# One recorded order for all five engines after the first transform of a spectral filter and two-layer expert kernel

## The chip, the cores and the metric

The kernel runs on one core of a Trainium2 chip. The metric is the device time in microseconds (us) of one execution. TensorE (PE) multiplies matrices into PSUM; VectorE (DVE), ScalarE (ACT) and GpSimd (POOL) do the elementwise work; SyncE (SP) and ACT issue nearly all transfers. Each engine takes its instructions from its own queue in order.

## The reference

Eight sequences of 3072 tokens with 256 channels go through three stages (cut to what matters):

```python
X = np.fft.rfft(x, axis=1)                        # spectral filter, per batch and channel
y = np.fft.irfft(X * (filt_r + 1j * filt_i), n=3072, axis=1)
y_prev = shift y by one token                      # zero at the start
xk = mu_k * y + (1 - mu_k) * y_prev;  xr = mu_r * y + (1 - mu_r) * y_prev
x2 = sigmoid(xr @ w_r) * (np.maximum(xk @ w_k, 0) ** 2 @ w_v)      # d_ff 1024
h = maximum(x2 @ w1, x2 @ w2, x2 @ w3)                             # 768 wide
out = h @ w_out
```

## The kernel before

**Stages.** The first batch's transform (`fft_first`) stands alone at the start, on an order written by hand. After it the tokens are worked through in 64 chunks of 384 tokens (eight a batch) and 32 pairs of chunks. Every large product is made of three matmuls on high and low parts, 384 columns wide.

- `kv(i)` is the list of steps for chunk i: `r_mm` (12 matmuls and a sigmoid), eight times `k_mm` (6 matmuls; then ACT relu `kr`, DVE square, ACT cast `khi`, POOL subtraction `klo`) and, three steps behind (`LAG`), eight times `v_mm` (6 matmuls that read `khi`, `klo` and a streamed weight tile `ws`). `x2` multiplies by the gate.
- `y_load` and `y_mm` fetch a chunk of transformed data and make its inputs `xh`, `xl`.
- `combos(p)` makes seven combinations of a pair; `second(p)` is nine `block`s of seven products (`one` to `seven`, 3 matmuls each, PSUM tiles `pb`, `pa`, `pe`) that feed a running maximum `m`, split into `hh`. `o_mm` (6 matmuls of 256 columns) multiplies `hh` by w_out, six calls for each third of the blocks; three `po` tiles gather them over the pair.
- `fft(b)` is the transform of batch b = 1 to 7, done beside the chunks of batch b-1: 17 steps `pa` that load x, add or subtract on DVE and call `a_mm1` or `a_mm0`, then steps that load (`b_load`), multiply (`b_mm`), filter on ACT, DVE and POOL (`b_filt`), multiply back (`c_mm`) and store (`c_out`) for six groups u. These matmuls use a quarter of the array each (64 by 64), in `quarters`: 126 groups over the run (42 of `b_mm`, 42 of `c_mm`, 28 of `a_mm1`, 14 of `a_mm0`), each with two PSUM tiles. Ahead of a group DVE copies one element into each of its two PSUM tiles (line 493), so that DVE takes the wait for the bank.
- During the first chunks `wjobs2` converts the weights of the expert stage (ACT, DVE, POOL, matmuls `ps`, stores).

**Order.** `drive` deals the steps of `fft(b)` out among the steps of the chunks by weights written beside each step. What it yields is only a program order: a list scheduler with a timeline of its own then sets each engine's order, from priorities and a general cost model; only the matmuls of `quarters` are raised in priority and chained. PSUM has eight banks in one pool `ps`, which all matmul tiles share.

Of the kernel before, what the change touches and what calls it, by code (L numbers as in the profile page):

```python
# [1 line left out]

# [214 lines left out]
def drive(main, side, total_main, total_side):  # L217

    done_m = 0.0
    done_s = 0.0  # L220
    i = 0
    for w, fn in main:
        fn()
        done_m += w
        while i < len(side) and done_s * total_main < done_m * total_side:
            side[i][1]()
            done_s += side[i][0]
            i += 1
    while i < len(side):
        side[i][1]()  # L230
        i += 1
# [3 lines left out]
def tile_spectral_moe(ctx: ExitStack, tc, x, xr, xz, filt, ones, wa, wa1, wi, wbc, wb1, wc1, filt1, filt0, mu, w_k, w_v, w_r, w1, w2, w3, w_out, out):  # L235
# [17 lines left out]
    fp = ctx.enter_context(tc.tile_pool(name="fp", bufs=2))  # L253
    ws = ctx.enter_context(tc.tile_pool(name="ws", bufs=10))
    dp = ctx.enter_context(tc.tile_pool(name="dp", bufs=2, space=bass.MemoryType.DRAM))
# [3 lines left out]
    ps = ctx.enter_context(tc.tile_pool(name="ps", bufs=8, space=bass.MemoryType.PSUM))  # L259
# [176 lines left out]
    def fft(b):  # L436
# [6 lines left out]
        pieces = []  # L443

# [42 lines left out]
        def quarters(o, of, whole=False):  # L487

            last = None
            for y in range(2):  # L490
                _, d = of(y, 1, 1)
                d = d[:1, 0, :1] if whole else d[:1, :1]
                i = nc.vector.tensor_copy(o[y][y * H : y * H + 1, 0, :1], d)
                if y:
                    tc.add_manual_dep(i.ins, last, ORDER_ONLY, reason="banks")
                last = i.ins.name
            last = None
            for k in range(1 if whole else 2):
                for y in (1, 0):
                    for x in range(2):  # L500
                        w, d = of(y, x, k)
                        to = o[y][x * H : x * H + H] if whole else o[y][x * H : x * H + H, k]
                        with tc.high_priority():
                            i = mm(to, w, d, k == 0, True, True, (y * H, x * H))
                        if last is not None:
                            tc.add_manual_dep(i.ins, last, ORDER_ONLY, reason="quarters")
                        last = i.ins.name
# [5 lines left out]
        NBS = NG // 2  # L513
        for u in range(len(jobs) + 1):
            def pa(u=u):
                if u == 0:
                    jobs[0][0](*jobs[0][2:])
                if u + 1 < len(jobs):
                    jobs[u + 1][0](*jobs[u + 1][2:])
                if u < len(jobs):  # L520
                    jobs[u][1](*jobs[u][2:])
                if u:
                    _, what, t, x = jobs[u - 1]
                    if x and what is a_diff:
                        a_mm1(t)
                    elif x and t % 2:
                        a_mm0(t - 1)
            pieces.append((0.53, pa))
# [53 lines left out]
        for u in range(NU4 + 2):  # L582
            def pb(u=u):
                if u < NU4:
                    b_load(u)
                if 1 <= u <= NU4:
                    b_mm(u - 1)
                    b_filt(u - 1, 0)
            def pb2(u=u):
                if 1 <= u <= NU4:  # L590
                    b_filt(u - 1, 1)
            def pc(u=u):
                if u >= 2:
                    c_mm(u - 2)
                    c_out(u - 2, 0)
            def pc2(u=u):
                if u >= 2:
                    c_out(u - 2, 1)
            pieces.append((0.4, pb))
            pieces.append((0.7, pb2))  # L600
            if u == 0:

                pieces.append((7.7, lambda: None))
            pieces.append((0.4, pc))
            pieces.append((0.7, pc2))
        return pieces
# [183 lines left out]
    mp = ctx.enter_context(tc.tile_pool(name="mp", bufs=2))  # L790
# [214 lines left out]
    def kv(i, before=()):  # L1005

        u = []
        before = list(before)
        at = [later(wv_d[f // 2][:, f % 2], 2, C) for f in range(NF)]
        add = lambda w, fn, *a: u.append((w, lambda: fn(*a)))  # L1010

        def some(n):
            while before and n:
                u.append(before.pop(0))
                n -= 1

        if i > 0:
            add(1.95, r_mm, i)
        direct = i + 1 < NTOT and (i in (0, 2) or i % 2 == 1 and i != 3)
        for f in range(NF):  # L1020
            add(0.98, k_mm, i, f)
            some(1)
            if f == 0 and direct:
                add(0.0, y_load, i + 1)
            if f == 4 and direct:
                add(1.3, y_mm, i + 1)
            if f >= LAG:
                add(0.98, v_mm, i, f - LAG, at[f - LAG])
        for f in range(NF - LAG, NF):
            add(0.98, v_mm, i, f, at[f])  # L1030
        some(len(before))
        if i == 0:
            add(1.95, r_mm, i)
        add(0.0, x2, i)
        return u

    def second(p):

        u = []
        add = lambda w, fn, *a: u.append((w, lambda: fn(*a)))  # L1040
        nb = NB
        i = 2 * p + (3 if p else 4)
        todo = []

        at = [{} for _ in range(nb)]

        def ask(k, a, e):
            i = later(wu_d[k][:, a:e], e - a, 2, P)
            at[k].update({n: (i, n - a) for n in range(a, e)})

        for k in range(nb + 1):
            if k < nb:
                ask(k, 0, 2)
            if k:
                ask(k - 1, 4, 5)
            if k < nb:
                ask(k, 2, 4)
            if k:
                ask(k - 1, 5, 7)
        for k in range(nb):  # L1060
            if k == 1 and i < NTOT:
                add(0.0, y_load, i)
            if k and k % 3 == 0:
                todo = [lambda q=q, fq=k // 3 - 1: o_mm(p, fq, q) for q in range(2 * NTB)]
            now = block(p, k, at[k])
            for n, fn in enumerate(now):

                u.append((0.52, fn))
                if n in (0, 2, 3) and k:
                    u.append((0.52, late.pop(0)))  # L1070
                if todo and n in ((3,), (0, 2, 3), (0, 1))[k % 3]:
                    u.append((0.71, todo.pop(0)))
                if n == 3:
                    break
            late = now[4:]
            if k == nb - 3 and i < NTOT:
                add(1.3, y_mm, i)
        for fn in late:
            u.append((0.52, fn))
        return u, [(0.71, lambda q=q: o_mm(p, NU // 2 - 1, q)) for q in range(2 * NTB)]  # L1080


    kv0 = kv(0)
# [15 lines left out]
    units = kv0 + kv(1) + kv(2) + [(0.0, lambda: combos(0))] + kv(3)  # L1099
    marks, cuts = {}, {}  # L1100
    before2 = len(units)
    s, left = second(0)
    units += s
    units.append((0.0, lambda: combos(1)))
    for p in range(1, NPAIR):
        i = 2 * p + 2
        if i < NTOT:
            if i % NCH == 0:
                marks[i // NCH] = len(units)
            units += kv(i, left if p == 1 else ())  # L1110
        s, left = second(p)
        units += s
        if i + 1 < NTOT:
            if (i + 2) % NCH == 0:
                cuts[i // NCH] = len(units)
            end = i + 2 == NTOT
            units += kv(i + 1, () if end else left)
            units.append((0.0, lambda p=p: combos(p + 1)))
            if end:
                units += left  # L1120
# [3 lines left out]
    for k, fn in enumerate(wjobs2):  # L1124
        units.insert(min(3 + int(k * (before2 - 3) / (NB + 1.5)), before2 + 10 + 3 * (k - NB)) + k, (0.0, fn))
    units.insert(20, (0.0, lambda: tc.keep_in_program_order(nc.gpsimd.dma_start(wa_s, wa))))
    n2 = len(wjobs2) + 1

    lead = before2 + n2
    starts = [0] + [marks[b] + n2 for b in range(1, B)]  # L1130
    ends = starts[1:] + [len(units)]
    for b in range(B):
        part = units[starts[b] : ends[b]]
        if b + 1 < B:
            side = fft(b + 1)
            cut = cuts[b] + n2 - starts[b]
            if b == 0:
                for _, fn in part[:lead]:
                    fn()
                part, cut = part[lead:], cut - lead  # L1140
            drive(part[:cut], side, sum(w for w, _ in part[:cut]), sum(w for w, _ in side))
            for _, fn in part[cut:]:
                fn()
        else:
            for _, fn in part:
                fn()
# [47 lines left out]
```

## Time and profile before

| | |
|---|---|
| median of 3 runs | 3155.18 us (3153.65 to 3156.64) |
| the profiled execution | 3154.04 us |
| its span in the trace | 3152.3 us |
| first transform ends, weights of the chunks warm up | 81 us |
| last matmul starts | 3146.14 us |
| transfers | 660 MB, mean 209 GB/s |

The profiled execution is 1.1 us under the median, and 1.7 us over its span. A busy share of PE is to be read with care: matmuls overlap, and a matmul's recorded length (340 ns) is near twice the step from one to the next, so a PE that waits a little still shows as busy.

### The profile page before, as it was taken

How to read it: one execution, taken by the hardware profiler on the slowest of the kernel's cores; microseconds unless marked ns; L12 is line 12 of the kernel's file. 1: busy time of each engine (PE TensorE's matmuls, PEld its weight loads, DVE VectorE, ACT ScalarE, POOL GpSimd, SP SyncE). 2: the span in 40 equal slices, each digit the busy share in tenths (PEclk: the TensorE clock that was granted, in tenths of full speed). 3: DMA queues.
4: the chain of work that ended last, by engine and by line, in shares of the span. 5: the costliest groups of instructions: out<-in, count | busy, mean ns of one | idle time of the engine just before them, and what ended most of it. 6: DMA issues, size and time to landing. Idle time of an engine off the chain costs nothing.

```text
span 3152.3 us, 56835 instructions
## 1 busy us (share of the span) xinstructions
PE 3075.5 (98%) x19816; PEld 2914.4 (92%) x19816; DVE 1872.8 (59%) x3313; ACT 1877.1 (60%) x3901; POOL 1626.9 (52%) x1416
## 2 busy tenths in 40 slices
PE   8799999999999999999999999999999999999998
PEld 5788989999989989999999998999999999999998
DVE  7875675466655666456655576545665456545554
ACT  6555655566555665556656566565655566655554
POOL 5433654457544565446645465455654466544443
PEclk9899999999999999999999999999999999999999
DMA  7777677666776666767767577775776666555554
GB/s 240 228 243 237 206 264 241 193 184 215 252 228 196 202 218 216 245 179 221 233 214 217 174 228 233 227 223 167 226 258 228 189 187 213 169 164 171 160 166 122
DMA packets 385195, 660.24 MB, mean 209 GB/s; under 512 B 41473, under 2 KB 150177, under 8 KB 384625
## 3 DMA queue, kind: packets, MB, share of 16 engines
q1 hardware_dynamic: 319584, 581.94, 59.9%
q10 hardware_dynamic: 64720, 72.52, 6.7%
q8 instruction: 160, 2.62, 0.3%
q0 software_dynamic: 608, 2.16, 0.2%
q14 instruction: 123, 1.00, 0.1%
HBM read 573.75 MB, written 82.71 MB: 208 GB/s over the span
## 4 chain that ended last, share of the span: by engine, by line
PE 78%; DVE 9%; DMA 4%; POOL 4%; issue 3%; ACT 2%; SPq 0%; ACTq 0%; POOLq 0%; DVEq 0%
PE pb L262 18%; PE pv L262 13%; PE pk L262 12%; PE po L262 12%; PE pe L262 8%; PE pa L262 5%; PE pr L262 4%; PE py L262 3%; POOL klo L290 2%; PE pc L262 1%; DMA ws<-wud 1%; DMA xr<-in_xr 1%; DVE filt L559 1%; DVE sc L887 1%; DVE m L970 1%
## 5 line engine op out<-in xcount | busy, mean ns | idle before, releaser
L290 POOL TENSOR_TENSOR hh<-m,hh 128x384 fp32r<-128x384 f32 x384 | 407.5, 1070 | 829.9 <-ACT hh L289 629.2
L262 PE MATMUL pb<-x,ws 128*128 128x384 f32 x3456 | 768.9, 340 | 13.5 <-DMA ws<-wud 6.7
L290 POOL TENSOR_TENSOR klo<-kr,khi 128x384 fp32r<-128x384 f32 x492 | 522.7, 1070 | 311.6 <-ACT khi L289 287.4
L262 PEld LDWEIGHTS pb<-x,ws 128*128 128x128 f32 x3456 | 597.1, 189 | 56.4 <-issue 13.6
L855 DVE SCALAR_TENSOR_TENSOR kr<-pk,kr 128x384 f32<-128x384 f32 x512 | 281.0, 553 | 365.3 <-ACT kr L854 363.4
L262 PE MATMUL pv<-khi,ws 128*128 128x384 f32 x2048 | 483.4, 338 | 14.2 <-ACT khi L289 11.3
L262 PE MATMUL po<-wo_hi,hh 128*128 128x256 f32 x2304 | 480.6, 283 | 4.8 <-ACT hh L289 4.0
L262 PEld LDWEIGHTS po<-wo_hi,hh 128*128 128x128 f32 x2304 | 389.0, 189 | 12.4 <-ACT hh L289 7.3
L262 PE MATMUL pe<-x,ws 128*128 128x384 f32 x1728 | 390.0, 339 | 2.4 <-DVE sc L969 1.2
L289 ACT CAST khi<-kr 128x384 fp32r<-128x384 f32 x512 | 261.1, 513 | 215.2 <-DVE kr L855 200.0
L262 PEld LDWEIGHTS pv<-khi,ws 128*128 128x128 f32 x2048 | 358.6, 188 | 30.8 <-ACT khi L289 16.5
L262 PE MATMUL pk<-xh,wk_hi 128*128 128x384 f32 x1024 | 341.4, 338 | 3.6 <-ACT xh L289 3.3
L262 PE MATMUL pk<-xh,wk_lo 128*128 128x384 f32 x1024 | 343.9, 336 | 0.0
L262 PE MATMUL pk<-xl,wk_hi 128*128 128x384 f32 x1024 | 343.1, 335 | 0.0
L854 ACT ACTIVATE kr<-pk 128x384 f32<-128x384 f32 x512 | 249.9, 490 | 124.1 <-POOL klo L290 57.7
L262 PE MATMUL po<-wo_lo,hh 128*128 128x256 f32 x1152 | 315.9, 281 | 0.0
L262 PE MATMUL pv<-klo,ws 128*128 128x384 f32 x1024 | 300.1, 339 | 8.5 <-POOL klo L290 6.7
L262 PEld LDWEIGHTS pe<-x,ws 128*128 128x128 f32 x1728 | 298.3, 189 | 10.6 <-DVE m L962 4.9
L970 DVE TENSOR_TENSOR m<-sc,m 128x384 f32<-128x384 f32 x384 | 275.7, 721 | 9.0
L289 ACT CAST hh<-m 128x384 fp32r<-128x384 f32 x384 | 191.9, 514 | 148.6 <-DVE m L970 86.5
L290 POOL TENSOR_TENSOR xl<-xm,xh 128x768 fp32r<-128x768 f32 x126 | 233.2, 1864 | 88.3 <-ACT xh L289 87.8
L923 ACT COPY v<-pb 128x384 f32<-128x384 f32 x288 | 139.1, 483 | 159.9 <-PE pb L262 156.8
(137 smaller groups left out, 5476.3 us busy)
## 6 DMA issues: line engine op xcount, KB each, us to landing
ws<-wud SPq DMA_DIRECT2D x864, 256.0 KB, 3.4
ws<-wvd SPq DMA_DIRECT2D x512, 256.0 KB, 3.6
filt<-in_filt SPq DMA_DIRECT2D x84, 512.0 KB, 5.3
ws<-wud SPq DMA_DIRECT2D x288, 128.0 KB, 3.4
xz<-in_xz SPq DMA_DIRECT2D x56, 512.0 KB, 5.6
cin<-s SPq DMA_DIRECT2D x128, 192.0 KB, 3.7
out_dram<-osb ACTq DMA_DIRECT2D x192, 128.0 KB, 3.1
xr<-in_xr SPq DMA_DIRECT2D x56, 384.0 KB, 5.0
```

What stands on the lines that cost most here:

```text
L262: return nc.tensor.matmul(o, lhsT=wgt, rhs=rhs, start=start, stop=stop, skip_group_check=more, tile_position=at)
L289: nc.scalar.copy(hi, src)
L290: (lo_eng or nc.gpsimd).tensor_tensor(lo, src, hi.bitcast(F32), ALU.subtract)
L559: nc.vector.tensor_tensor(fi[e], q[a], fi[e], ALU.mult)
L854: nc.scalar.activation(r, p, AF.Relu)
L855: nc.vector.scalar_tensor_tensor(r, p, 0.0, r, ALU.max, ALU.mult)
L887: eng.tensor_tensor(t, a, b, ALU.subtract)
L923: nc.scalar.copy(st[to], st[of])
L970: nc.vector.tensor_tensor(m, c, m, ALU.max)
```

## The change

From the end of the first transform on, the kernel's instructions are no longer handed over when they are written. A recorder takes each call of the five engines, and the tiles are stand-ins with names; which call must follow which is worked out from the elements that they touch. Then `play` runs a model of the engines three times: `cost` gives each call a length, `plan` gives each call other than a matmul the latest time at which its first reader can do without it, `run` takes PE's calls strictly as written and lets each other engine take, of its calls that are ready and whose tile is free, the one with the earliest such time. The calls are then made in the order of their modelled starts, and all five engines are kept in that order.

With it the written order is different in these places: the last three `v_mm` of a chunk, `x2` and (where due) `combos` are dealt out among the first steps of the next stage (`mixed`); `o_mm` starts a block later and comes two to a block; `y_mm` of the next chunk stands after step 2 in place of 4 (from chunk 4 on); the steps of the transforms stand at fixed places (`steps`), with `b_mm(u)` and `c_mm(u-1)` side by side and `b_load` a step ahead; the one-element copies, the raised priority and the chain in `quarters` are gone.

```diff
-def drive(main, side, total_main, total_side):
-...
+class Order:
+    OVERLAP = dict(ACT=100, DVE=80, POOL=42)
+    ISSUE = dict(SP=367, ACT=570, POOL=900)
+    SHARE = dict(DVE=0.40, POOL=0.77)
+    WAKE = 55
+...
+    def cost(self, o, out, ins, k):
+...
+        if e == "PE":
+            if k.get("tile_position") is not None:
+                o.quarter = True
+                o.holds, o.takes_ns = n // 2, 595
+            elif k["lhsT"].dtype == F32R:
+                o.holds = 4 + n * 0.4455 - (2 if n == 384 else 0)
+...
+        elif e == "DVE":
+            both = len([v for v in ins if np.prod(v.shape[1:]) > 1]) > 1
+            o.takes_ns = 150 + n * 1.065 if psum or both else 65 + n * 0.7
+            o.shared = not psum
+...
+    def plan(self, times):
+        t, last = {}, 0.0
+        late = [0.0] * len(self.calls)
+        for o in reversed(self.calls):
+            if o.engine == "PE":
+                last = late[o.k] = times[o.k]
+                continue
+            w = min((late[j] for j in o.after), default=last + 4000.0)
+            late[o.k] = min(w - self.WAKE, last + 30000.0) - o.takes_ns - (2200 if o.kind == "dma" else 0)
+        return late
+...
+        def mix(t):
+            both = len(share) == 2 and all(s[3] for s in share.values())
+            for e, s in share.items():
+                s[0] -= (t - s[2]) * s[1]
+                s[2] = t
+                s[1] = self.SHARE[e] if both else 1.0
+...
+            for i, (_, k) in enumerate(ready[e]):
+                if room(self.calls[k]):
+                    del ready[e][i]
+                    begin(self.calls[k], t)
+                    break
+...
+        for _ in range(rounds):
+            start = self.run(self.plan(times))
+            times = {o.k: start[o.k] for o in self.calls if o.engine == "PE"}
+        for k in sorted(range(len(start)), key=lambda k: (start[k], k)):
+            self.calls[k].call()
...
         def quarters(o, of, whole=False):
...
-            for y in range(2):
-                _, d = of(y, 1, 1)
-                d = d[:1, 0, :1] if whole else d[:1, :1]
-                i = nc.vector.tensor_copy(o[y][y * H : y * H + 1, 0, :1], d)
-...
-                        with tc.high_priority():
-                            i = mm(to, w, d, k == 0, True, True, (y * H, x * H))
-...
+                        mm(to, w, d, k == 0, True, True, (y * H, x * H))
...
+        def bc_step(u):
+            if u < NU4:
+                b_mm(u)
+            if u:
+                c_mm(u - 1)
+            if u + 1 < NU4:
+                b_load(u + 1)
+            for z in range(2):
+                if u < NU4:
+                    b_filt(u, z)
+            for z in range(2):
+                if u:
+                    c_out(u - 1, z)
...
+        tail = [lambda f=f: v_mm(i, f, at[f]) for f in range(NF - LAG, NF)]
...
+        return u, tail + [lambda: x2(i)]
...
+        for k in range(nb + 1):
+            if k and k % 3 == 0:
+                todo = todo + [lambda q=q, fq=k // 3 - 1: o_mm(p, fq, q) for q in range(2 * NTB)]
+            n = 0 if k < 4 else 2
+            mine, todo = todo[:n], todo[n:]
+...
+                u += late[:2] + [two, three] + mine[:1] + late[2:] + [four] + mine[1:]
...
+    def mixed(tail, u, first=1, step=2):
+        u = list(u)
+        for n, fn in enumerate(tail):
+            u.insert(min(first + n * (step + 1), len(u)), fn)
+        return u
...
+            places = [("kv", i, f) for f in (0, 2, 4, 6)] + [("second", p, k) for k in (4, 5, 6, 7, 8)] + [("kv", i + 1, f) for f in range(8)]
+            bc = [("kv", i + 2, 1), ("second", p + 1, 3), ("kv", i + 3, 2), ("kv", i + 3, 7), ("kv", i + 4, 3), ("second", p + 2, 3), ("kv", i + 5, 3)]
...
+    ctx.enter_context(tc.manual_schedule(engines={E.PE, E.Activation, E.DVE, E.Pool, E.SP}))
+    order.play()
```

## Rows read from the trace of the kernel before

**Rows 1.** Page, part 1: busy us, share of the span, instructions.
```profile
PE 3075.5 (98%) x19816; PEld 2914.4 (92%) x19816; DVE 1872.8 (59%) x3313; ACT 1877.1 (60%) x3901; POOL 1626.9 (52%) x1416
```

**Rows 2.** Timeline of PE from 2820 us: start, us, what, count.
```profile
2820.75 1.92 PE L262 MATMUL py<-wi_s,cin 96*128 96x96 f32 x16
2822.46 0.60 PE L262 MATMUL pv<-khi,ws 128*128 128x384 f32 x2
...
2823.59 0.33 PE L262 MATMUL pk<-xh,wk_hi 128*128 128x384 f32 x1
...
2824.63 0.28 PE L262 MATMUL po<-wo_hi,hh 128*128 128x256 f32 x1
...
2825.34 0.51 PE L262 MATMUL pv<-khi,ws 128*128 128x384 f32 x2
```

**Rows 3.** Timeline of PE around one group of quarter matmuls.
```profile
1426.39 0.51 PE L262 MATMUL pv<-klo,ws 128*128 128x384 f32 x2
1426.83 1.09 PE L262 MATMUL pb<-xb,wbc 64*64 64x256 f32 x16
1427.85 0.61 PE L262 MATMUL pv<-khi,ws 128*128 128x384 f32 x2
1428.30 0.34 PE L262 MATMUL pv<-klo,ws 128*128 128x384 f32 x1
```

**Rows 4.** Timeline of PE: first matmuls after the first transform, last matmul.
```profile
81.26 1.76 PE L262 MATMUL pz<-wk_hi 128*128 128x384 f32 x8
...
3146.14 0.28 PE L262 MATMUL po<-wo_hi,hh 128*128 128x256 f32 x1
```

**Rows 5.** Waits of PE, 500 to 2800 us: us in total, times, longest.
```profile
PE pv L262 <- POOL klo L290: 4.5, 6, 0.9
PE pv L262 <- ACT khi L289: 4.2, 7, 0.7
PE pb L262 <- DMA ws<-wud: 2.9, 4, 1.3
PE po L262 <- ACT hh L289: 2.2, 4, 0.6
...
PE py L262 <- DVE m L966: 0.2, 1, 0.2
```

**Rows 6.** Waits of PE, 104 to 500 us.
```profile
PE pv L262 <- ACT khi L289: 7.1, 5, 3.6
PE pb L262 <- DMA ws<-wud: 3.8, 1, 3.8
PE pv L262 <- POOL klo L290: 2.2, 5, 0.9
...
PE pa L262 <- DVE pa L493: 0.2, 1, 0.2
```

**Rows 7.** Timeline of PE around one wait; in brackets the idle time and its releaser.
```profile
1537.99 0.86 PE L262 MATMUL pv<-khi,ws 128*128 128x384 f32 x4
1539.58 0.62 PE L262 MATMUL pv<-klo,ws 128*128 128x384 f32 x2 [0.73 <-POOL klo L290]
1540.04 0.88 PE L262 MATMUL pv<-khi,ws 128*128 128x384 f32 x4
```

**Rows 8.** Stretches: us, then busy PE, PEld, DVE, ACT, POOL, PE clock, DMA share, GB/s.
```profile
100.00:200.00 100.00, 91.33 (x587) 88.59 (x587) 85.92 (x136) 57.95 (x117) 47.44 (x35) 0.98 0.68 216
...
300.00:400.00 100.00, 94.02 (x621) 88.11 (x620) 58.63 (x105) 57.61 (x118) 55.28 (x48) 0.97 0.72 212
...
2422.00:2799.00 377.00, 375.27 (x2459) 360.46 (x2458) 215.40 (x384) 231.79 (x485) 204.41 (x178) 1.00 0.64 197
2800.00:3080.00 280.00, 280.00 (x1762) 279.91 (x1761) 147.19 (x249) 160.27 (x347) 138.40 (x125) 1.00 0.53 159
```

**Rows 9.** Groups of DVE by line: busy us, mean ns, idle before and its releasers.
```profile
L560 DVE TENSOR_TENSOR filt<-pb,filt 128x512 f32<-128x512 f32 x84 | 58.1, 692 | 1.2
...
L493 DVE COPY pb<-xb 1x1 f32<-1x1 f32 x84 | 13.0, 155 | 44.5 <-ACT gate L845 25.8 <-ACT co L578 15.7 <-ACT osb L996 1.1
```

**Rows 10.** Line 290 by operation: ns min/median/max, first and last start.
```profile
L290 POOL TENSOR_TENSOR x<-sc,x x64: 1006/1326/2311, 164.4 to 3097.0; 128x384 fp32r<-128x384 f32 x64
L290 DVE TENSOR_TENSOR x<-sc,x x64: 541/1357/1372, 168.9 to 3096.7; 128x384 fp32r<-128x384 f32 x64
```

More of the change, by code (lines that the diff above doesn't have):

```diff
@@ L1 @@
+import bisect
+import heapq
 from contextlib import ExitStack
+from types import SimpleNamespace
 import numpy as np
@@ L442, in fft @@
         st = {}
-        pieces = []
         def x_load(t, x):
@@ L512, in fft, with a_step @@
             jobs += [(x_load, a_sum, t + n, x) for n in range(2) for x in range(2)]
[L513 to L528, printed above, removed]
+        def a_step(u):
+            if u == 0:
+                jobs[0][0](*jobs[0][2:])
+            if u + 1 < len(jobs):
+                jobs[u + 1][0](*jobs[u + 1][2:])
+            if u < len(jobs):
+                jobs[u][1](*jobs[u][2:])
+            if u:
+                _, what, t, x = jobs[u - 1]
+                if x and what is a_diff:
+                    a_mm1(t)
+                elif x and t % 2:
+                    a_mm0(t - 1)
+            if u == len(jobs):
+                b_load(0)
         def b_load(u):
@@ L580, in c_out @@
             nc.scalar.dma_start(s2.rearrange("h m r g c -> (h m r) g c")[:, g : g + 2, :], o)
-        for u in range(NU4 + 2):
-            def pb(u=u):
-                if u < NU4:
[L585 to L606, printed above, removed]
+        def bc_step(u):
[6 more added lines that the diff above has]
+            for z in range(2):
+                if u < NU4:
+                    b_filt(u, z)
+            for z in range(2):
+                if u:
+                    c_out(u - 1, z)
+        return a_step, bc_step
     def fft_first(pp, jobs, more):
@@ L1003, in tile_spectral_moe, with at_place, kv @@
     NTOT = B * NCH
-    def kv(i, before=()):
-        u = []
+    plan = {}
+    def at_place(*place):
+        for fn in plan.get(place, ()):
+            fn()
+    def kv(i, before=(), after=None):
         before = list(before)
         at = [later(wv_d[f // 2][:, f % 2], 2, C) for f in range(NF)]
-        add = lambda w, fn, *a: u.append((w, lambda: fn(*a)))
+        u = []
+        add = lambda fn, *a: u.append(lambda: fn(*a))
         def some(n):
@@ L1059, in second @@
                 ask(k - 1, 5, 7)
-        for k in range(nb):
+        for k in range(nb + 1):
             if k == 1 and i < NTOT:
-                add(0.0, y_load, i)
+                u.append(lambda: y_load(i))
             if k and k % 3 == 0:
[L1064 to L1083, printed above, removed]
+                todo = todo + [lambda q=q, fq=k // 3 - 1: o_mm(p, fq, q) for q in range(2 * NTB)]
+            n = 0 if k < 4 else 2
+            mine, todo = todo[:n], todo[n:]
+            if k < nb:
+                u.append(lambda k=k: at_place("second", p, k))
+                one, two, three, four, *rest = block(p, k, at[k])
+                u.append(one)
+                u += late[:2] + [two, three] + mine[:1] + late[2:] + [four] + mine[1:]
+                late = rest
+                if k == nb - 3 and i < NTOT:
+                    u.append(lambda: y_mm(i))
+            else:
+                u += mine[:1] + late[:2] + mine[1:] + late[2:]
+                left = todo
+        return u, left
+    kv0 = sum(kv(0), [])
     y_load(0)
@@ L1108, in tile_spectral_moe @@
             if i % NCH == 0:
-                marks[i // NCH] = len(units)
-            units += kv(i, left if p == 1 else ())
+                if i // NCH + 1 < B:
+                    units.append(lambda b=i // NCH + 1: transform(b))
+            u, t = kv(i, left if p == 1 else ())
+            units += mixed(tail, u)
+            tail = t
         s, left = second(p)
-        units += s
+        units += mixed(tail, s, 2)
+        tail = []
         if i + 1 < NTOT:
-            if (i + 2) % NCH == 0:
-                cuts[i // NCH] = len(units)
             end = i + 2 == NTOT
-            units += kv(i + 1, () if end else left)
-            units.append((0.0, lambda p=p: combos(p + 1)))
+            u, t = kv(i + 1, () if end else left)
+            units += u
+            tail = t + cm(p + 1)
             if end:
-                units += left
+                units += tail + left
+                tail = []
         else:
@@ L1124, in tile_spectral_moe @@
     for k, fn in enumerate(wjobs2):
[L1125 to L1146, printed above, removed]
+        units.insert(min(3 + int(k * (before2 - 3) / (NB + 1.5)), before2 + 10 + 3 * (k - NB)) + k, fn)
+    units.insert(20, lambda: nc.gpsimd.dma_start(wa_s, wa))
+    for fn in units:
+        fn()
+    E = mybir.EngineType
+    ctx.enter_context(tc.manual_schedule(engines={E.PE, E.Activation, E.DVE, E.Pool, E.SP}))
+    order.play()
 def kernel(x, filt_r, filt_i, moe_mu_k, moe_mu_r, moe_w_k, moe_w_v, moe_w_r, moe2_w1, moe2_w2, moe2_w3, moe2_w_out):
```

407 lines of the change are left out of this document (364 added, 43 removed).

## The prediction

> **What bounds the kernel now.** I read the page's busy shares first: PE 98%, the others 52 to 60% [rows 1]. A matmul's recorded length hides short waits, so next I read the timeline of PE where nothing disturbs it, to get the true step from one matmul to the next [rows 2]: six of 384 columns from 2823.59 to 2824.63 us give 0.1733 us each, six of 256 columns to 2825.34 give 0.118, sixteen of `py` to 2822.46 give 0.107. A group of quarter matmuls takes 1.02 us [rows 3]. With the counts of the code this makes a floor for PE after the first transform: 64 chunks of 108 and 32 pairs of 189 matmuls are 12960 x 0.1733 = 2246; `o_mm` 32 x 108 = 3456 x 0.118 = 408; `py` 1056 x 0.107 = 113; 252 `ps` matmuls, taken at 0.11 (an estimate from `py`), 28; 126 quarter groups x 1.02 = 129 (the eight-matmul groups taken at the same length); the eight warm-up matmuls 1. Together 2925 us. PE takes from 81.26 to 3146.26 us for it [rows 4], 3065 us. So the order on PE and its waits cost **140 us**; no change of order can give more, since no matmul is removed.
>
> Where do they lie? Third view, PE's waits by stretch. From 500 to 2800 us ten kinds of wait, 38 in number, sum to 19.1 us [rows 5]; from 104 to 500 us fourteen kinds, 22 waits, sum to 21.4 us [rows 6]. Each costs more than the idle time shown. In one example [rows 7] four matmuls from 1537.99 should hand over after 0.69 us and do so after 1.59: 0.90 lost where 0.73 is shown; and the two matmuls after it take 0.46 in place of 0.35. So a wait costs its idle time and 0.28 us: 19.1 + 38 x 0.28 = **29.7 us** steady, 21.4 + 22 x 0.28 = **27.6 us** early. Entering a quarter group costs 0.09 us (0.44 for two matmuls) and the step behind it 0.10 [rows 3]: 126 x 0.19 = **24 us**. What is left, 140 - 29.7 - 27.6 - 24 = **59 us**, is waits too short to show, the two ends of the run, and matmuls at the half clock.
>
> The decisive view is the stretches [rows 8]. From 2800 to 3080 us, the last batch, which has no transform beside it, PE is busy 280.00 of 280 us, while DVE, ACT and POOL are busy 53, 57 and 49%. In the 377 us before it they are busy 57, 61 and 54%, hardly more, yet PE loses time. So the side engines do not lack capacity there; they do the right work at the wrong moment. That is what an order can mend. Between 100 and 200 us it is otherwise: DVE is busy 85.92 of 100 us, and an order can mend only part.
>
> **The change part by part.**
>
> *Steady waits.* Of the 29.7 us, the 17 waits of `pv` on `klo` and `khi` and of `po` on `hh` [rows 5] are 10.9 + 17 x 0.28 = 15.7 us. The written order removes their cause: the last three `v_mm` of a chunk now stand among steps of the next stage, 1 to 2 us of matmuls between each, and `o_mm` comes a block later (21 matmuls x 0.1733 = 3.6 us). The four waits for `ws` (2.9 + 1.1 = 4.0 us) hang on SP's queue, where the 256 KB loads of `ws` stand among the transform's loads; the change puts all of them in the order of modelled need, so a load that waits for its buffer is passed by those that need not. The other 17 (10.0 us) are PSUM banks and maxima that DVE or ACT gave free late. Bounds: 29.7 us if all go, as in the last batch; below nothing if the fixed order makes more (a rival, below). I take four fifths, **24 us**, nearer to the last batch's row, since the load differs so little.
>
> *Early waits.* 27.6 us, and 3 us that the half clock costs between 300 and 400 us (granted clock 0.97 of 100 us [rows 8]) behind the one wait of 3.8 us for `ws` [rows 6]. That load is a matter of SP's order alone. The rest are `khi` and `klo` behind the weight conversion on a DVE at 86%. Earliest need lets a square pass a conversion, but the `ps` matmuls stand at fixed places in PE's order and wait for conversions. Bounds 0 and 31; I take six tenths, **18 us**.
>
> *Quarter groups.* `b_mm(u)` and `c_mm(u-1)` side by side for u = 1 to 5 in seven transforms merge 35 pairs of groups: 35 x 0.19 = **7 us**. Nothing else on PE's own work changes.
>
> *The one-element copies.* 252 of them at 0.155 us are 39 us of DVE; the 84 for `pb` also held the DVE queue idle for 44.5 us, mostly until ACT emptied a bank [rows 9], with the squares and maxima queued behind. All this is off PE's path (DVE is at 59%) and its worth is in the terms above. The wait itself does not vanish: now the first quarter matmul waits for the bank, and PE's whole queue stands behind it. If the cover fails, this is the price that the slower rival takes.
>
> *Short waits.* Of the 59 us I take a quarter, **15 us**: most of the span has transforms beside it and should come near the undisturbed steps; the start's chain of loads, the tail and half-clock stretches stay. Bounds 0 and 31 (about half, the share that I estimate to be short waits).
>
> *Moved transfers.* The loads of x and of the filters are issued by SP at places that the model chooses; `b_load` of the next group goes out a step ahead of its use. SP's order was the scheduler's before and is the model's now, so the sign is open: I put it at nothing. As a loss I bound it by one wait like the early one of 3.8 us [rows 6] in each of seven transforms, 27 us, which would leave 3117, inside the range.
>
> *Port.* DVE and POOL slow each other when both read two SBUF tiles: `x` on DVE takes 541 ns at best and 1357 in the median, on POOL 1006 and 1326 [rows 10]. Both stretch, and the planner's shares say just that (541/0.40 = 1352, 1006/0.77 = 1306), so its times for such work should hold. The Trainium skill, SBUF — State Buffer, "SBUF: two separate sides", says otherwise: the shared port pair is an exclusive lock and the loser blocks fully. By that rule the DVE operation would end after 541 + 1006 = 1547 ns, 0.19 us later than planned, and if each of the 32 pairs lost that once on PE, 6 us of the gain would be gone (3096); the medians here speak for sharing.
>
> Sum: 24 + 18 + 7 + 15 = 64 us. From the profiled execution's 3154.0 us this gives **3090 us**, and 3091 from the median, which is 1.1 us higher. All upper bounds together, 30 + 31 + 7 + 31 = 99, give 3055; two or three us more are to be had at the tail, so the low end is 3052.
>
> **The rivals.**
>
> *The plan misjudges (3129, from 3120 to 3147).* All five queues are fixed by a model. Where it errs by a few tenths of a us, an in-order engine waits for one input with ready work behind it. Then short waits and most steady ones come back elsewhere, and only the merged groups and a part of the early waits remain: 7 + 18 = 25 us. For it: 60% load on ACT, with queue upon queue [rows 1]. Against it: the last batch's row. Chance 0.15.
>
> *It does nothing that can be measured.* The scheduler's order was fixed too, also from a model; gains and new waits may cancel. 3154, within 0.2% (6 us, about what a measurement of this kernel can tell from no change). Chance 0.07.
>
> *Slower: the merged groups starve for PSUM banks.* A merged step needs four free banks at once where two did before; `pv` holds two, `po` up to three, and `pk` or `pb` two more, of eight. Priority on ACT and DVE goes by who needs the data, and nobody needs `c_out` soon, so banks are emptied last. The price is DVE's share of `b_filt`, six operations of 0.69 us [rows 9], 4.1 us a step: 35 x 4.1 = 144 us against the 64 gained, so 3234. It decides from 64/35 = 1.8 us a step. Against it: the places chosen lie mostly where `po` or `pv` is not held, and ACT is idle 40% of the time. The Trainium skill, TensorEngine Tiling (Array Packing), "PSUM Bottleneck", warns of this: tiling speeds up PE, not the emptying of PSUM, so the copies may become the bottleneck. No row before shows four banks wanted at once. Chance 0.16.
>
> **How the numbers follow.** The forecast has the remaining 0.62, of which I put 0.02 below 3052. The range from 3052 to 3150 holds 0.60 of it, the misjudged plan's 0.15 and 0.04 of the no-change case: 0.79. Faster by over 0.2%: 0.62 + 0.15 = 0.77; within: 0.07; slower: 0.16.
>
> **What would show it.** Right: PE's waits from 500 to 2800 us fall from 38 to under ten, those for `klo`, `khi` and `hh` gone; 91 quarter groups in place of 126, runs of 32 matmuls among them; `pv` waits before 300 us halved; DVE's 252 one-element copies gone and its busy time some 39 us lower. Wrong: waits of `pc` or `pb` (quarter) for ACT `co` or DVE `filt` would be the bank rival; many scattered waits under 0.5 us, or waits for `ws`, the misjudged plan. If the waits go and the time does not, my floor is wrong.

## The result and the profile after

The changed kernel takes 3175.7 us (median of 4 runs, 3172.8 to 3177.5) where the kernel before takes 3154.7: a ratio of 1.0065, with a 95% interval from 1.0047 to 1.0082. It is 21 us slower where 64 us less were forecast.

The page of the changed kernel, part 1, against [rows 1]: PE has 9 us less recorded work and waits longer; DVE has 252 instructions less and yet 55 us more.

```profile
span 3171.1 us, 56339 instructions
...
PE 3066.8 (97%) x19816; PEld 2929.2 (92%) x19816; DVE 1927.7 (61%) x3061; ACT 1904.8 (60%) x3901; POOL 1671.8 (53%) x1416
```

PE's waits from 500 to 2800 us, all seven kinds (us in total, times, longest), against [rows 5]. Every call now goes through the recorder, so all lines read L241; go by the tiles.

```profile
PE pb L241 <- DMA xb<-s1a: 30.3, 6, 5.9
PE pb L241 <- ACT pa L241: 12.5, 11, 1.5
PE po L241 <- POOL hh L241: 10.3, 12, 0.9
PE pk L241 <- DVE kr L241: 2.7, 6, 0.5
PE pv L241 <- DVE filt L241: 2.4, 6, 0.4
PE pb L241 <- DMA xb<-s1b: 0.8, 1, 0.8
PE pb L241 <- ACT u L241: 0.5, 3, 0.2
```

What the forecast said would go is gone: no wait for `klo`, `khi`, `ws`, or for `hh` from ACT is left. But 59.5 us of others stand in the place of 19.1. Half of them is one kind: six waits of about 5 us, one in each of the transforms of batches 2 to 7, for `xb`, the data that the second part of a transform reads back from DRAM. The two next largest come at the same places of each transform: `po` for `hh` on POOL is new, and `pb` for the copy `pa` on ACT has grown from this line of the kernel before:

```profile
PE pb L262 <- ACT pa L928: 1.7, 6, 0.3
```

Early on the change does what was forecast. PE's waits from 104 to 500 us are seven kinds, 10 waits and 11.3 us, where 22 waits and 21.4 us were [rows 6]; the largest:

```profile
PE pb L241 <- ACT pa L241: 3.5, 3, 1.8
PE pe L241 <- ACT ao L241: 1.9, 1, 1.9
PE pb L241 <- DMA ws<-wud: 1.8, 1, 1.8
```

In stretches (columns as in [rows 8]) PE is busy 99.65 of the 100 us from 100 to 200, where it was busy 91.33, though DVE is now busy 97.66 us of them; the stretch from 2800 us on, without a transform, is as undisturbed as before.

```profile
100.00:200.00 100.00, 99.65 (x655) 99.06 (x655) 97.66 (x152) 63.68 (x128) 49.83 (x37) 0.97 0.71 228
...
2800.00:3080.00 280.00, 280.00 (x1765) 279.19 (x1765) 148.33 (x249) 162.40 (x345) 139.05 (x122) 1.00 0.55 164
```

**The wait for `xb`, followed back.** The timeline of one of the six, ACT first, then SP, then PE (start, us, what, count; ACTq and SPq are transfers as the queue issues them):

```profile
941.23 1.09 ACTq L241 DMA_DIRECT2D s1b<-ao  x2
...
945.21 0.59 ACT L241 COPY ao<-pa 128x512 f32<-128x512 f32 x1 [0.82 <-DMA s1b<-ao]
...
946.90 0.37 ACTq L241 DMA_DIRECT2D s1a<-ao  x1
...
950.05 0.32 SPq L241 DMA_DIRECT2D ws<-wud  x1
950.47 2.44 SPq L241 DMA_DIRECT2D xb<-s1a  x4
...
943.51 1.09 PE L241 MATMUL pa<-xs,wa_s 64*64 64x256 f32 x16
944.53 0.44 PE L241 MATMUL pr<-xh,wr_hi 128*128 128x384 f32 x1
...
950.73 0.34 PE L241 MATMUL pk<-xh,wk_lo 128*128 128x384 f32 x1
956.02 2.09 PE L241 MATMUL pb<-xb,wbc 64*64 64x256 f32 x16 [4.96 <-DMA xb<-s1a]
```

The last product of the first part, two PSUM tiles, is done at 944.53. It comes out of PSUM into `ao` tiles, of which there are two; each must be stored before it can be filled again, and the copy at 945.21 starts as the first of the two earlier stores has landed. The last store goes out at 946.90 and lands at 949.04. The loads stand on SP's queue behind a load of `ws`, which waits for PE to free its buffer, and go out at 950.47; the data that PE needs is there at 956.0. In two of the six places the loads follow the landing of the last store within 0.1 us; in the other four they come 0.7 to 1.4 us after it, behind such a `ws` load, 4.7 us in all. PE reaches `b_mm(0)` at 950.9 and, being kept in the written order, stands for 5 us with its whole queue behind it. The last step of the first part stands at step 7 of chunk i+1 and `b_mm(0)` at step 1 of chunk i+2: the next thing but one. Between them lie 36 matmuls, 6.4 us; from the end of the last product to the data it takes 11.0 to 12.4 us in the six places.

**The waits for `pa`, followed back.** The timeline behind one merged group, DVE first, then ACT, then PE:

```profile
1084.49 0.68 DVE L241 SCALAR_TENSOR_TENSOR filt<-pb,filt 32x512 f32<-32x512 f32 x1
1085.92 0.68 DVE L241 TENSOR_TENSOR filt<-pb,filt 32x512 f32<-32x512 f32 x1 [0.75 <-ACT v L241]
1087.34 0.69 DVE L241 TENSOR_TENSOR filt<-pb,filt 128x512 f32<-128x512 f32 x1 [0.74 <-ACT v L241]
...
1085.21 0.68 ACT L241 ACTIVATE v<-pb,sg_s 32x512 f32<-32x512 f32 x1 [0.88 <-DVE filt L241]
1086.63 1.38 ACT L241 ACTIVATE v<-pb,sg_s 32x512 f32<-32x512 f32 x2 [0.75 <-DVE filt L241]
1088.04 0.46 ACT L241 COPY pa<-pb 128x384 f32<-128x384 f32 x1
...
1083.31 1.09 PE L241 MATMUL pb<-xb,wbc 64*64 64x256 f32 x16
1084.22 1.04 PE L241 MATMUL pc<-yz,wbc 64*64 64x256 f32 x16
1085.19 0.79 PE L241 MATMUL pb<-x,ws 128*128 128x384 f32 x3
...
1088.56 0.61 PE L241 MATMUL pb<-x,ws 128*128 128x384 f32 x2 [1.53 <-ACT pa L241]
```

DVE and ACT take turns, at 1084.49, 1085.21, 1085.92, 1086.63 and 1087.34, each waiting for the other. Yet `filt` and `v` (lines 556 to 560 of the kernel before) exchange nothing here. Both only read `pb`, and neither reads what the other writes; DVE's first two operations even read other partitions (0 to 63) than ACT's two (64 to 127). The waits are semaphores in the program. My reading is that the framework lets only one engine at a time into a PSUM tile, in the order in which the calls were made; the recorder counts two reads as free of each other, so its plan makes the calls in turns. Each handoff holds both queues, ACT's copy `pa` with them, and PE behind that.

### The profile page after: what moved, and what is told of

Its sections match the earlier page's. It is cut to its first block, busy times and chain, and to the rows that moved or that the text cites. A ratio compares the mean times of both kernels' runs of the same rounds, so it can differ in the third digit from the quotient of the medians.

```text
span 3171.1 us, 56339 instructions
## 1 busy us (share of the span) xinstructions
PE 3066.8 (97%) x19816; PEld 2929.2 (92%) x19816; DVE 1927.7 (61%) x3061; ACT 1904.8 (60%) x3901; POOL 1671.8 (53%) x1416
## 3 DMA queue, kind: packets, MB, share of 16 engines
q1 hardware_dynamic: 319584, 581.94, 59.5%
## 4 chain that ended last, share of the span: by engine, by line
PE 87%; DMA 4%; ACT 3%; DVE 3%; POOL 2%; issue 1%; ACTq 0%; SPq 0%; POOLq 0%; DVEq 0%
PE pb L241 20%; PE pk L241 16%; PE pv L241 15%; PE po L241 12%; PE pe L241 9%; PE pa L241 6%; PE pr L241 4%; PE py L241 4%; ACT v L241 1%; DVE filt L241 1%; POOL hh L241 1%; PE ps L241 1%; DMA xb<-s1a 1%; DMA wci<-in_wc 1%; PE pc L241 1%
## 5 line engine op out<-in xcount | busy, mean ns | idle before, releaser
L241 POOL TENSOR_TENSOR hh<-m,hh 128x384 fp32r<-128x384 f32 x384 | 435.4, 1152 | 747.2 <-ACT hh L241 667.8
L241 PE MATMUL pb<-x,ws 128*128 128x384 f32 x3456 | 751.5, 339 | 23.0 <-ACT pa L241 17.1
L241 POOL TENSOR_TENSOR klo<-kr,khi 128x384 fp32r<-128x384 f32 x492 | 537.7, 1101 | 343.7 <-ACT khi L241 311.5
L241 PEld LDWEIGHTS pb<-x,ws 128*128 128x128 f32 x3456 | 600.2, 188 | 57.1 <-ACT pa L241 30.4
L241 DVE SCALAR_TENSOR_TENSOR kr<-pk,kr 128x384 f32<-128x384 f32 x512 | 281.9, 553 | 412.8 <-ACT kr L241 404.3
L241 PE MATMUL pv<-khi,ws 128*128 128x384 f32 x2048 | 525.7, 337 | 2.4 <-DVE filt L241 2.4
L241 PE MATMUL po<-wo_hi,hh 128*128 128x256 f32 x2304 | 500.4, 282 | 13.2 <-POOL hh L241 12.7
L241 PEld LDWEIGHTS po<-wo_hi,hh 128*128 128x128 f32 x2304 | 391.3, 189 | 16.2 <-POOL hh L241 15.5
L241 PE MATMUL pe<-x,ws 128*128 128x384 f32 x1728 | 395.2, 336 | 1.9 <-ACT ao L241 1.9
L241 ACT ACTIVATE kr<-pk 128x384 f32<-128x384 f32 x512 | 251.1, 490 | 207.2 <-PE pk L241 121.7
L241 PEld LDWEIGHTS pv<-khi,ws 128*128 128x128 f32 x2048 | 366.9, 189 | 8.7 <-DMA xb<-s1a 4.5
L241 PE MATMUL pk<-xh,wk_hi 128*128 128x384 f32 x1024 | 352.5, 344 | 5.5 <-DVE kr L241 2.9
L241 PE MATMUL pv<-klo,ws 128*128 128x384 f32 x1024 | 344.5, 336 | 1.4 <-POOL klo L241 1.4
L241 PE MATMUL pk<-xl,wk_hi 128*128 128x384 f32 x1024 | 344.6, 337 | 0.1
L241 PE MATMUL pk<-xh,wk_lo 128*128 128x384 f32 x1024 | 344.2, 336 | 0.0
L241 ACT CAST khi<-kr 128x384 fp32r<-128x384 f32 x512 | 261.3, 513 | 131.6 <-DVE kr L241 113.3
L241 POOL TENSOR_TENSOR xl<-xm,xh 128x768 fp32r<-128x768 f32 x126 | 239.7, 1916 | 185.7 <-ACT xh L241 183.2
L241 PE MATMUL po<-wo_lo,hh 128*128 128x256 f32 x1152 | 324.2, 281 | 0.0
L241 ACT CAST hh<-m 128x384 fp32r<-128x384 f32 x384 | 187.9, 514 | 195.4 <-DVE m L241 193.5
L241 DVE TENSOR_TENSOR m<-sc,m 128x384 f32<-128x384 f32 x384 | 297.4, 775 | 5.8
L241 PEld LDWEIGHTS pe<-x,ws 128*128 128x128 f32 x1728 | 295.8, 188 | 5.1 <-ACT ao L241 4.4
L241 ACT COPY u<-pb 128x384 f32<-128x384 f32 x288 | 138.1, 479 | 175.5 <-PE pb L241 173.3
```

The costliest lines, as they stand in the source:

```text
L241: o = SimpleNamespace(engine=engine, call=lambda: call(*map(real, a), **{n: real(v) for n, v in k.items()}), what=call.__name__, k=len(sel ...
```

## The experiments

Theory: the plan works, and two things that it does not hold cost more than it gains: a way through DRAM that is longer than PE's written order leaves room for, and an order between readers of one PSUM tile. Rival: an order fixed by any model errs all over, and each wait seen is one instance of it.

**Move the read-back.**

```diff
-            bc = [("kv", i + 2, 1), ("second", p + 1, 3), ...
+            bc = [("kv", i + 2, 5), ("second", p + 1, 3), ...
```

> The changed kernel with one place moved: for batches 2 to 7 the first transform matmuls on stored data (b_mm(0)) stand at step 5 of chunk i+2 in place of step 1, some 8 us later on PE. Theory (store and load again): PE stood 30.3 us in six waits of about 5 us for xb, because the data had been stored to DRAM only just before; with the restart, 32 us go and the time is 3143 (3139 to 3147). Rival (the fixed order errs everywhere): PE waits elsewhere, for instance in the steps behind, and no more than half is gained: 3160 to 3176.

3130.0 us, ratio to the kernel before 0.9917 (0.9900 to 0.9935): this line alone makes the change a gain. It is worth 45.7 us, 14 more than the 32 of its waits, and the time is 9 us below the theory's range. The wait for `xb` is gone, the other waits stayed as they were: 12.4 us from 500 to 2800 us for `pa`, 10.1 for `hh`. The rival is out for this part. Where most of the 14 us come from is seen in the stretch around the first of the six, here of the changed kernel and, in the second fence, of this one:

```profile
569.00:580.00 11.00, 6.89 (x38) 6.08 (x39) 4.19 (x8) 4.59 (x8) 3.55 (x3) 0.69 0.89 215
```

```profile
569.00:580.00 11.00, 11.00 (x74) 10.24 (x73) 10.41 (x15) 9.27 (x20) 9.86 (x8) 1.00 1.02 244
```

The granted clock in the 11 us is 0.69: behind the wait PE ran at the lower of its two levels (1.2 in place of 2.4 GHz) for a while, though it had work. The first quarter group above shows it: 16 matmuls take 2.02 us, from 956.02 to 958.04, where 1.02 is usual [rows 3]. It is so behind all six: over the 13 to 15 us around each the granted clock is 0.74 to 0.88.

**Half the distance.**

```diff
-            bc = [("kv", i + 2, 1), ("second", p + 1, 3), ...
+            bc = [("kv", i + 2, 3), ("second", p + 1, 3), ...
```

> The changed kernel (3175.7) with b_mm(0) moved by two steps of chunk i+2, to step 3, where the first experiment moved it by four. Some 3 to 5 us of matmuls now lie ahead of it, so of each wait of 5 us for xb 0 to 2 us stay. Theory (the wait also brought a spell of half clock behind it, 31 us in all six, worth 15 us): short waits bring no half clock, so far more than the idle time saved is gained: 3131 to 3143. Rival (the 14 us that the first experiment gained over the waits came from where step 5 lies): the gain is the idle time alone, 3145 to 3156.

3138.3 us, 37 less, where the idle time for `xb` shrank by 26, from 30.3 to 4.4 us in three waits, longest 2.1. So most of what the wait cost beyond its length went with it. The distance is now 60 matmuls, 10.5 us; where PE still waits the data comes 11.3 to 12.8 us after the last product. The first experiment's distance, 84 matmuls or 14.7 us, is more than that, and so is the 90 matmuls that batch 1 has in the changed kernel, where PE does not wait. The lower clock is not gone wholly, as the theory had it: around the first of the six places the clock is whole, but behind one wait of 1.7 us at 1328 us it is not (both stretches of this kernel), while behind the longest, of 2.1 us at 2461 us, it is (1.00):

```profile
569.00:580.00 11.00, 10.50 (x70) 9.82 (x69) 9.87 (x14) 8.83 (x18) 7.99 (x7) 1.00 1.01 240
...
1325.00:1336.00 11.00, 9.32 (x54) 8.65 (x54) 8.57 (x11) 7.57 (x15) 7.66 (x7) 0.84 1.03 235
```

The size comes out in two parts. The waiting is 30.3 us and six restarts of 0.28, about 32 us. Behind the waits, sixty matmuls took 1.8 to 2.7 us longer than at their usual steps, 12.5 us in all six; behind the two waits of this run that left the clock whole it is 0.25 us each. So the lower clock cost some 11 us (an estimate), and 43 of the 45.7 us are accounted for.

**Reprice transfers in the plan.** Is it the queues that store and load too late, because the plan takes transfers for short?

```diff
-                took = wire + 1900 - t
+                took = wire + 3900 - t
...
-            ... - (2200 if o.kind == "dma" else 0)
+            ... - (4200 if o.kind == "dma" else 0)
```

> The changed kernel (3175.7) with another price in the planner: a transfer takes 3.9 us after its issue in place of 1.9, and 4.2 in place of 2.2 where the latest times are worked out. Theory (PE's own written place is the defect, so no order of the queues mends it): the six waits for xb stay within a us each, 3168 to 3182. Rival (the queues issue stores and loads late because the plan takes transfers for too short): the waits halve and the half clock behind them goes, 3135 to 3155.

3169.8 us, within the theory's range, but the waits for `xb` did not stay as it had them, nor did they halve as the rival had it; they grew by half:

```profile
PE pb L241 <- DMA xb<-s1a: 44.0, 6, 7.6
PE pb L241 <- ACT pa L241: 9.3, 15, 0.9
```

In this run the loads go out within 0.1 us of the landing of the last store in all six places, so SP's queue does not hold them. What grew lies on ACT: the first copy that reuses an `ao` tile starts 1.6 to 2.4 us after the landing that frees it, where it was 0.1 us, since the plan now takes that landing to be later. A plan with the dearer price could not use it for a gain, since PE's order is no part of what it may change. (The profiled execution took 3174.9 us, of six between 3168.3 and 3175.8, so the trace does not tell where the median's 6 us less come from.)

**Tell the recorder of the PSUM tile.**

```diff
+            bank = t is not None and t.space == "PSUM" and k < o.k and self.calls[k].engine != o.engine
-            if meet and not both and (w or write) and not (dram and write):
+            if (bank or meet and not both and (w or write)) and not (dram and write):
```

> The changed kernel with one rule added to the recorder: two engines that touch the same PSUM tile follow each other in the written order, also where both only read. Theory (bank handoffs that the plan did not know): ACT and DVE took turns on one pb tile, five handoffs in a row, and held up the copies to pa and the maxima; the waits of pb for ACT pa (12.5 us, 11) and of pv and pk for DVE filt and kr (5.1 us, 12) go, with restarts 24 us, and perhaps part of the 10.3 us for POOL hh: 3140 to 3158 against 3176. Rival (ACT and DVE are simply too busy there): the waits stay and the time is 3170 to 3180.

3156.3 us: 19.4 less than the changed kernel, and the same as the kernel before (1.0003). ACT's waits in the changed kernel, and in the second fence all that is left of them for `v`:

```profile
ACT v L241 <- PE pb L241: 211.8, 203, 6.3
...
ACT v L241 <- DVE filt L241: 23.3, 33, 1.1
```

```profile
ACT v L241 <- PE pb L241: 205.3, 199, 6.9
```

No wait of `v` for DVE's reads is left, as the reading says; DVE still waits for ACT's reads (52.4 us in 31 waits, before 24.9 in 38), now in one piece in place of turns. PE's waits for `pa` from 500 to 2800 us fall from 12.5 us to 2.5, and those for `hh` from 10.3 to 5.5. Those of `pk` and `pv` for DVE were expected to go too and stayed (5.5 us in 12). All of PE's waits from 104 to 2800 us fall by 18.1 us and by six in number, 19.8 us with the restarts, near the 19.4 measured. The time lies inside the theory's bounds; ACT and DVE had the capacity. That it is the framework which orders the two readers is inferred from this; no run tests that by itself.

**Both.** The two edits together.

> Both edits. If both theories hold they add up: 32 + 18 to 35 us less than 3176, so 3109 to 3126, faster than the kernel before. If the fixed order errs everywhere, the sum is well short of that: over 3140.

3104.6 us, ratio 0.9833 (0.9818 to 0.9848), 50 us faster than the kernel before; 71 us less than the changed kernel, where the two edits alone sum to 65. It is the best version found. All of PE's waits from 500 to 2800 us:

```profile
PE po L241 <- POOL hh L241: 5.5, 12, 0.5
PE pk L241 <- DVE filt L241: 2.9, 6, 0.7
PE pv L241 <- DVE filt L241: 2.0, 6, 0.3
PE pr L241 <- DVE kr L241: 0.5, 1, 0.5
PE pb L241 <- ACT pa L241: 0.2, 1, 0.2
```

**The written order alone.** The changed kernel with the recorder off, the manual schedule left out, and `quarters` as before.

```diff
-    order.on = True
...
-    ctx.enter_context(tc.manual_schedule(engines={E.PE, E.Activation, E.DVE, E.Pool, E.SP}))
-    order.play()
```

> The written order of the changed kernel alone: nothing is recorded, the list scheduler orders the engines as in the kernel before, and the quarter groups have their one-element copies, raised priority and chain again. Theory (two defects, each of its own): the scheduler may fill the wait for xb with other matmuls, so this lies near the kernel before, 3135 to 3165. Rival (to record and plan is itself the loss): this keeps all the gain of the written order and lies under 3125.

3216.1 us, 1.0188 (1.0172 to 1.0204): slower than both expected. No wait for `xb` is left, as the theory had it, but the largest others are 21.7 us of `pk` for DVE `filt` and 13.4 of `pv` for `khi` (500 to 2800 us). The list scheduler makes less of the new written order than of the old one. So the loss of the change is not in recording and planning, which on the same written order is worth 40 us with its two gaps and 112 with them closed (the place of `b_mm(0)` among these).

**Written first in place of needed first.** In the kernel with both edits `plan` returns the number of the call as its latest time.

```diff
-        return late
+        return [float(k) for k in range(len(late))]
```

> The kernel with both edits (3104.6), where the other engines take of their ready calls the one written first, not the one needed earliest. Theory (the earliest need is what removes the early and steady waits): PE waits for klo, khi and bank copies come back, 3125 to 3200. Rival (a fixed order made by any model of the run does it, need or not): 3100 to 3112.

3293.7 us, 189 more and 94 beyond the theory's range. The waits for `khi` are back, and those for `klo` (14.9 us in 17), and the copies `u` and `pa` on ACT come far later than before:

```profile
PE pb L241 <- ACT u L241: 35.8, 23, 1.6
PE pb L241 <- ACT pa L241: 32.0, 24, 2.5
PE pv L241 <- ACT khi L241: 20.2, 12, 2.7
```

A fixed order alone does not bring the gain; without the earliest need it loses more than it had gained.

**Merged groups apart again.** In the kernel with both edits, `c_mm` and `c_out` one place ahead of `b_mm`.

```diff
...
         for u, place in enumerate(bc):
-            put(place, lambda u=u: bc_step(u))
+            if u:
+                put((*place[:2], place[2] - 1), lambda u=u: bc_step(u, "c"))
+            if u + 1 < len(bc):
+                put(place, lambda u=u: bc_step(u, "b"))
```

> The kernel with both edits (3104.6), with each c_mm and c_out one place ahead of b_mm instead of behind it in the same place, so that 126 quarter groups stand alone again. Theory (the merged groups are worth what entering and leaving costs): 35 x 0.19 = 7 us more, 3109 to 3114. Rival (merging crowds PSUM banks, ACT and DVE, and that costs more than it saves): at or under 3104.

3105.5 us: no difference. On PE a merged pair saves even more than was thought, since 32 matmuls in a row take 1.88 us (1083.31 to 1085.19 in the timeline above) where twice 16 take 2.04: 35 x (0.19 + 0.16) = 12 us. But apart, the steady waits are 4.9 us in 18 where they were 11.1 in 26:

```profile
PE pb L241 <- ACT v L241: 3.4, 12, 0.3
PE pv L241 <- POOL klo L241: 1.5, 6, 0.3
```

With 0.28 us a wait this gives back 6.2 + 8 x 0.28 = 8 us. So crowding costs nearly what merging saves.

**Apart in the second stages only**, the same edit for the places that are named `second`.

> The kernel with both edits (3104.6), with c_mm one place ahead of b_mm only where the place is in a second stage (14 of the 35 pairs), and side by side in chunks. Theory (a merged pair saves some 0.35 us of PE, and in the second stages crowding takes back more, as po waits for POOL hh): 14 x 0.35 = 5 us lost, 9 us of waits gained, 3098 to 3103. Rival (the waits do not hang on the crowding there): 3106 to 3111.

3112.5 us (3106.3 to 3115.6), worse than either. The waits of `po` for `hh` did go, but as many came for `pa` and `v`; the rival's range ends at 3111, and what the rest hangs on was not followed.

**Low parts last in `o_mm`.** In the kernel with both edits, the two matmuls that read `hl` behind the four that read `hh`.

```diff
         for f in range(2):
...
             mm(o, hh, oh, fq == 0 and f == 0 and k % 2 == 0, False, True)
             mm(o, hh, ol, False, False, True)
-            mm(o, hl, oh, False, last, True)
+        for f in range(2):
+            last = f == 1 and fq == NU // 2 - 1
+            mm(o, cs["h", fq, c, f][:, 1, s], wo[0][:, 2 * fq + f], False, last, True)
```

> The kernel with both edits (3104.6), and in each o_mm the two matmuls on the low part hl stand last, behind the four on the high part. Theory (the 14 waits of po for POOL hh, 7.4 us and 4 us of restarts, come from the low part being read 0.24 us after the high one): each wait shrinks by some 0.25 to 0.35 us, 3099 to 3102. Rival (the high part is late as well, or POOL has the next thing late): 3103 to 3106.

3105.6 us, no difference, and the twelve waits of `po` for POOL `hh` are still 5.5 us. What makes POOL late there stays open.

## Why the prediction was wrong, step by step

Between the forecast of 3091 us and the 3175.7 measured lie 85 us. The two gaps closed together make 71 of them: one in a term that was put at nothing, one in the largest term of the sum.

**Where PE loses, and the floor: right.** The waits that were priced fell as the forecast says and the kernel with both edits gains 50 us of the 64, inside the range of the forecast. With both edits PE's recorded work is 3050.3 us.

**Early waits, 18 us: right in the main.** 21.4 us in 22 waits became 11.3 in 10, so 10.1 + 12 x 0.28 = 13.5 us. The granted clock between 300 and 400 us is whole again (1.00 for 0.97), but between 200 and 300 us it is 0.98 where it was 1.00, so little comes from it. With both edits it is more: 5.4 us in 6 waits, so 16.0 + 16 x 0.28 = 20.5, and the 3 of the clock, which is now whole in both stretches.

**Steady waits, 24 us: the cures worked, the balance failed.** The 17 waits for `klo`, `khi` and `hh` from ACT and the four for `ws` are gone. In their place, beside `xb`, stand 29.2 us in 39 waits. I had reasoned that the side engines lack no capacity and so an order could only help. The capacity was there (ACT and DVE were at 60%), but I did not ask what the plan does not know. Its list of who must follow whom leaves out two readers of one PSUM tile, which the diff shows (`w or write`), and the kernel before hides, since its scheduler had put ACT's two reads ahead of DVE's three. Closing this gap is worth 19.4 us and brings the term, in the kernel with both edits, to 8.0 + 12 x 0.28 = 11 us, half of what was forecast.

**Moved transfers, put at nothing, at most 27 us of loss: the step that failed.** The 45.7 us are more than the whole bound. I priced SP's order, and that is at most 4.7 of the 30.3 us of idle time; with a dearer price in the plan the loads stood behind nothing and PE waited longer. What counts is how much of PE's written order lies between a store and the matmuls that read it back. I had noted that `b_load` goes out a step ahead, which holds for all but the first group: that one's load stands in the last step of the first part, behind its own stores. In the kernel before, an entry of weight 7.7 without work in the list of steps (in `fft`, between the load and `b_mm(0)`) kept the two apart: in its trace 609 matmuls, 98 us, lie between the last product of the first part and `b_mm(0)` of batches 2 to 7. The change removes the entry, the diff shows that, and I did not cost it. The written places leave 36 matmuls, 6.4 us, where the way through DRAM takes 11.0 to 12.4.

**Short waits, 15 us: not measured by itself.** With both edits 50 us were gained; less 23.5 of the early waits, 11 of the steady ones and some 4 of the merged groups, about 11 us are left for this term (an estimate by what is left).

**Quarter groups, 7 us: the size was off twice.** 91 groups as forecast, 12 us saved on PE (an estimate from the steps), about 8 given back in waits, and apart the kernel took 1 us more, within the scatter of its runs.

**The slower rival: the right side, not the mechanism.** I gave 0.16 to a loss behind the merged groups, from banks that are emptied too late, at 4.1 us a step. Waits behind merged groups there are, but no 1.8 us a step: apart or together, the time is the same, and the larger part went with the order between readers. I took a loss by a transfer for a bound inside the range, with no chance of its own.

**One-element copies, 39 us of DVE: gone, and DVE is busier all the same** (1927.7 us for 1872.8). Work with two inputs in SBUF meets POOL more often in the new order: of the 96 operations that make `x` on DVE, 38 were held by a running POOL operation in the kernel before and 80 are in the changed one. One such group in the kernel before and, in the second fence, in the changed one (busy us, mean ns):

```profile
L290 DVE TENSOR_TENSOR x<-gate,x 128x384 fp32r<-128x384 f32 x32 | 19.1, 596 | 0.0
```

```profile
L241 DVE TENSOR_TENSOR x<-gate,x 128x384 fp32r<-128x384 f32 x32 | 44.6, 1394 | 0.0
```

**Port: the planner's sizes were near, the reading of the rows was wrong.** I read the medians in [rows 10] as two engines that share, and added up 541 and 1006 ns of operations that mostly do not run beside each other. The timeline of the changed kernel tells more (DVE first, then POOL):

```profile
866.30 1.40 DVE L241 TENSOR_TENSOR x<-gate,x 128x384 fp32r<-128x384 f32 x1
...
866.27 1.02 POOL L241 TENSOR_TENSOR x<-sc,x 128x384 fp32r<-128x384 f32 x1
867.25 1.32 POOL L241 TENSOR_TENSOR klo<-kr,khi 128x384 fp32r<-128x384 f32 x1
```

POOL came first and kept its own pace (1.02 us); DVE, 0.03 us later, ended 0.41 us after POOL did; and the next POOL operation, begun while DVE still ran, is the one that stretches. Of the 86 operations making `x` on DVE that began while POOL ran, 80 ended 0.41 to 0.42 us after POOL's; the other six began in the last 0.02 us of it and took their usual 0.55. So one waits for the whole of the other, as the Trainium skill states (SBUF — State Buffer, "SBUF: two separate sides": an exclusive lock, the loser blocks fully), and this trace agrees. DVE's 1.40 us stay under the 1547 ns worked out in the prediction because it ends 0.41 us after POOL, not 0.54.

## What to carry to other kernels

Where one queue is kept as written and the others are planned around it, cost the written order as strictly as the plan: for each result that goes out to memory and comes back, add up copy, store, landing, load and landing (11 to 12 us here) and compare them with the work that stands between on the fixed queue (6.4 us). A planner is as good as its list of dependences: look in the trace for engines that wait for each other without exchanging data, and give the plan that rule. A wait has a price beyond its length; look at the granted clock behind it. And where two engines stretch each other, look at single operations, who began first and who ended when, before reading medians as sharing.

## What was not expected of the hardware

A wait of 5 us on PE cost 7.6 (45.7 us for six): the idle time, a restart of 0.28 us, and a spell at the lower clock behind it (granted 0.69 over the 11 us around the first). A DVE operation with two inputs in SBUF that begins while POOL runs ends 0.41 to 0.42 us after POOL's operation, 80 times of the 80 that POOL held up; POOL, being first, keeps its pace (1.02 us in the example). Quarter matmuls of two groups in one run take 1.88 us for 32, not twice 1.02.
